# Block attention with decay and a Gelu MLP on one core: a hand-ordered two-stream pipeline, with q, k, v loaded as float32 through SyncE's queue

## The chip, the core and the metric

The kernel runs on one core of a Trainium2 chip. A core has a matrix engine (TensorE: PE for matmuls, PEld for weight loads), three engines for elementwise work (VectorE or DVE, ScalarE or ACT, GpSimd or POOL) and SyncE (SP), which here only issues DMAs. Each engine works through its own instructions in order and waits on semaphores for the others. Matmul results land in PSUM, eight banks of 2 KB per partition; all other tiles lie in SBUF. DMAs are issued from a queue of SP or of POOL, and the loads from POOL may change the type on the way (float32 in memory, bf16 in SBUF).

The metric is the device time of one execution in microseconds, the median of several runs. A profile of one execution gives the spans and waits.

## What is computed

```python
def _attn_ref(q, k, v, lam):                 # q, k, v: (4, 8, 768, 64) float32
    ...
    for b in range(nb):
        sl = slice(b * block, (b + 1) * block)
        qb, kb, vb = (q[:, :, sl], k[:, :, sl], v[:, :, sl])
        intra = np.einsum('bhic,bhjc->bhij', qb, kb) * Dmask[None]
        intra = np.einsum('bhij,bhjd->bhid', intra, vb)
        inter = np.einsum('bhid,bhde->bhie', qb * lam_pow[None], kv_state)
        out[:, :, sl] = intra + inter
        rev_pow = lam[:, None, None] ** (block - 1 - pos[None, :, None])
        kb_dec = kb * rev_pow[None]
        kv_state = lam_block[None, :, None, None] * kv_state + np.einsum('bhsd,bhse->bhde', kb_dec, vb)

def _moe_ref(x, w_in, w_out):                # x: (3072, 512), w_in: (512, 2048), w_out: (2048, 512)
    h = x @ w_in
    g = 0.5 * h * (1.0 + erf(h * inv_sqrt2))
    return g @ w_out
```

Four batches of eight heads run causal attention with a decay `lam` per head, carried from block to block in a state of 64 by 64 per head. The heads' outputs, side by side, are the 512 features of 3,072 tokens, which pass a two-layer MLP with an exact Gelu.

## The kernel before

The kernel cuts a batch of 768 tokens into six chunks of 128. For a chunk, `attn_batch` multiplies q by `lam**pos` (`q_hat`, line 104) and k by `lam**-pos` (`k_hat`, line 105) on POOL, which makes the decay between two tokens a plain product. PE transposes both for pairs of heads (lines 112 and 113), DVE copies the two results out of PSUM (116, 117), PE forms the scores of eight heads (124), and DVE applies the causal mask while copying (`sc_m`, 130). Then PE makes the output, transposed, from the masked scores and v (135) and from q and the state of the earlier chunks (136), and ACT copies it into `xT_sb` (138), which holds the MLP's input for all tokens. The chunk's addition to the state is eight small matmuls (143), two DVE adds on the diagonal blocks (151, 152) and one DVE multiply by `lam**128` (153); two POOL memsets (149, 150) clear the blocks off the diagonal in the new state tile. The chain from `sc_m` to the output and the state to the next chunk is serial.

`moe_chunk` takes 256 tokens. For each of 16 blocks of 128 hidden features it runs four matmuls of 256 columns into `h_ps` (162; two buffers), a Gelu on ACT into `gT` (165), and two matmuls of 512 columns that add this block's share to two output banks (167). At the end ACT copies both banks (171) and SP stores them (172).

The program is traced batch by batch: attention of a batch, then its three MLP chunks. The Tile framework's scheduler orders the instructions of each engine by its own priorities and dependences, so attention of the next batch is moved among the matmuls of the MLP before. q, k and v of a batch come as three DMAs on POOL's queue (94 to 96), which turn float32 into bf16 and land in one tile per tensor; the tiles have two buffers. The weights are two more such DMAs, traced after batch 0 (180, 181). POOL therefore does the multiplies and issues all loads in one order, and SP only stores.

Of the kernel before, what the change touches and what calls it, by code (L numbers as in the profile page):

```python
# [8 lines left out]
F32 = mybir.dt.float32  # L10
BF16 = mybir.dt.bfloat16
I32 = mybir.dt.int32
ALU = mybir.AluOpType
# [4 lines left out]
def kernel(  # L18
# [10 lines left out]
    nc = tc.nc  # L29
# [3 lines left out]
    n_tokens = B * S  # L33
    C = 128
    NB = S // C
    assert d_model == H * D

    TOK = 256
    NK1 = d_model // 128
    NK2 = d_ff // 128  # L40
    NO = TOK // 128

    xT_pool = ctx.enter_context(tc.tile_pool(name="xTp", bufs=1))
    xT_sb = xT_pool.tile([128, d_model // 128, n_tokens], BF16)

    consts = ctx.enter_context(tc.tile_pool(name="consts", bufs=1))

    lam_b = consts.tile([128, H], F32)
    nc.sync.dma_start(lam_b, lam[None, :].to_broadcast((128, H)))
    ln_lam = consts.tile([128, H], F32)  # L50
    nc.scalar.activation(ln_lam, lam_b, ACT.Ln)
# [4 lines left out]

    lam_pos = consts.tile([128, H], F32)
    nc.vector.tensor_scalar(lam_pos, ln_lam, scalar1=pos, scalar2=None, op0=ALU.mult)
    nc.scalar.activation(lam_pos, lam_pos, ACT.Exp)

    lam_neg = consts.tile([128, H], F32)
    nc.vector.tensor_scalar(lam_neg, ln_lam, scalar1=pos, scalar2=-1.0, op0=ALU.mult, op1=ALU.mult)
    nc.scalar.activation(lam_neg, lam_neg, ACT.Exp)

    lam_blk = consts.tile([128, H, D], F32)
    nc.scalar.activation(lam_blk[:, :, :], ln_lam[:, :, None].to_broadcast((128, H, D)), ACT.Exp, scale=float(C))

# [3 lines left out]
    ident = consts.tile([128, 128], BF16)  # L71
    make_identity(nc, ident)
# [4 lines left out]
    lam_blk_hd = lam_blk.rearrange("p h d -> p (h d)")  # L77

    w_pool = ctx.enter_context(tc.tile_pool(name="w", bufs=1))
    w_in_t = w_pool.tile([128, d_model // 128, d_ff], BF16)  # L80
    w_out_t = w_pool.tile([128, d_ff // 128, d_model], BF16)

    qkv_pool = ctx.enter_context(tc.tile_pool(name="qkv", bufs=2))
    hat_pool = ctx.enter_context(tc.tile_pool(name="hat", bufs=2))
    work_pool = ctx.enter_context(tc.tile_pool(name="work", bufs=2))
    kv_pool = ctx.enter_context(tc.tile_pool(name="kv", bufs=2))
    g_pool = ctx.enter_context(tc.tile_pool(name="g", bufs=3))
    out_pool = ctx.enter_context(tc.tile_pool(name="outp", bufs=3))

    def attn_batch(b, psum):  # L90
        q_t = qkv_pool.tile([128, H, NB, D], BF16, tag="q")
        k_t = qkv_pool.tile([128, H, NB, D], BF16, tag="k")
        v_t = qkv_pool.tile([128, H, NB, D], BF16, tag="v")
        nc.gpsimd.dma_start(q_t, q[b].rearrange("h (so si) d -> si h so d", si=128))
        nc.gpsimd.dma_start(k_t, k[b].rearrange("h (so si) d -> si h so d", si=128))
        nc.gpsimd.dma_start(v_t, v[b].rearrange("h (so si) d -> si h so d", si=128))  # L96

        kv_state = kv_pool.tile([128, H * D], BF16)
        nc.vector.memset(kv_state, 0.0)

        for sb in range(NB):
            q_hat = hat_pool.tile([128, H, D], BF16, tag="qh")
            k_hat = hat_pool.tile([128, H, D], BF16, tag="kh")
            nc.gpsimd.tensor_mul(q_hat, q_t[:, :, sb, :], lam_pos_b)  # L104
            nc.gpsimd.tensor_mul(k_hat, k_t[:, :, sb, :], lam_neg_b)  # L105
            vb = v_t[:, :, sb, :]

            HP = H // 2
            qT_ps = psum.tile([128, HP * C], BF16, tag="qT")
            kT_ps = psum.tile([128, HP * C], BF16, tag="kT")  # L110
            for hp in range(HP):
# [102 lines left out]
```

## Time and profile before

| | |
|---|---|
| median of three runs | 297.76 us (297.51 to 354.67) |
| span of the profiled execution | 296.9 us |
| first matmul of the MLP (line 162) | starts at 37.1 us |
| last Gelu (line 165) | starts at 291.4 us |
| HBM read, written | 27.27 MB, 6.29 MB |
| DMA packets on POOL's queue | 76,512 (13.63 MB as landed) |
| mean granted TensorE clock | 0.960 |

The page of the profile covers one execution and has a span from the first to the last instruction; the time of a run is taken around the whole program, and the profiled execution's own time outside its span is not shown. In what follows, "idle before" is the time in which an engine had nothing running before an instruction, with the engine or DMA whose end released it. A matmul's duration includes its way through the array, so matmuls that start every 0.1 us each last longer than that; the distance between starts tells what PE can do. "L162" is line 162 of the kernel.

### The profile page before, as it was taken

The page shows a single profiled execution, that of the slowest core. Times are in us where ns is not written, and L with a number is a line of the kernel's source. Part 1 is how long each engine was busy: PE and PEld are TensorE (multiplying, and loading weights), DVE is VectorE, ACT ScalarE, POOL GpSimd, SP SyncE. Part 2 cuts the span into 40 slices and gives each one's busy share as a digit, 9 for nine tenths or more (in the row PEclk, how much of TensorE's full clock was granted, in tenths as well). Part 3 has the DMA queues.
Part 4 walks back from the last instruction along what each step waited for, and adds up shares of the span by engine and source line. Part 5 has one row for each costly group of instructions (what it writes and reads, how often), then busy time and mean ns, then how long its engine had stood idle before and what let it go on. Part 6 is the DMA issues. An engine that isn't in the chain of part 4 may idle for free.

```text
span 296.9 us, 5123 instructions
## 1 busy us (share of the span) xinstructions
PE 238.1 (80%) x2081; PEld 145.1 (49%) x2112; DVE 85.6 (29%) x150; ACT 103.8 (35%) x247; POOL 94.7 (32%) x119
## 2 busy tenths in 40 slices
PE   0037295999999789999999799999998789999893
PEld 0025162555555456655554555555555556555451
DVE  1037544400000679500000768300003778100000
ACT  4001221343344323353534223453533133453532
POOL 7474625847200778610000645300003531000000
PEclk9999997999999969999999879999999689999999
DMA  6996999999990194990010100010101000010101
GB/s 44 157 118 116 187 192 126 123 146 137 154 174 0 71 80 30 106 152 27 6 68 0 73 0 2 2 71 0 73 1 56 17 2 1 2 71 2 71 1 71
DMA packets 80135, 20.25 MB, mean 68 GB/s; under 512 B 74480, under 2 KB 76528, under 8 KB 80112
## 3 DMA queue, kind: packets, MB, share of 16 engines
q0 software_dynamic: 76512, 13.63, 67.0%
q1 hardware_dynamic: 3600, 6.30, 5.6%
q8 instruction: 16, 0.26, 0.4%
q14 instruction: 7, 0.06, 0.1%
HBM read 27.27 MB, written 6.29 MB: 113 GB/s over the span
## 4 chain that ended last, share of the span: by engine, by line
PE 60%; ACT 12%; DMA 9%; issue 7%; DVE 6%; POOL 4%; ACTq 1%; POOLq 0%
PE omps L167 32%; PE h_ps L162 16%; ACT gT L165 11%; DMA w_out_t<-in_moe_w_out_dram 5%; DMA k_t<-in_k_dram 4%; PE sc_ps L124 3%; PE out_ps L135 3%; DVE sc_m L130 3%; PE out_ps L136 2%; PE kT_ps L113 2%; POOL q_hat L104 1%; DVE kv_state_new L153 1%; PE qT_ps L112 1%; POOL k_hat L105 1%; PE kv_ps L143 1%
## 5 line engine op out<-in xcount | busy, mean ns | idle before, releaser
L162 PE MATMUL h_ps<-xT_sb,w_in_t 128*128 128x256 bf16 x768 | 116.4, 279 | 4.0 <-DMA w_in_t<-in_moe_w_in_dram 4.0
L167 PE MATMUL omps<-w_out_t,gT 128*128 128x512 bf16 x353 | 105.3, 386 | 15.8 <-ACT gT L165 4.4
L165 ACT ACTIVATE gT<-h_ps 128x256 bf16<-128x256 f32 x192 | 73.1, 384 | 127.2 <-PE h_ps L162 117.2
L162 PEld LDWEIGHTS <-w_in_t 128*128 128x128 bf16 x768 | 76.0, 100 | 42.1 <-DMA w_in_t<-in_moe_w_in_dram 4.3
L167 PEld LDWEIGHTS <-gT 128*128 128x128 bf16 x384 | 29.6, 98 | 50.6 <-ACT gT L165 35.9
L104 POOL TENSOR_TENSOR q_hat<-q_t,lam_pos 128x512 bf16<-128x512 bf16 x24 | 25.1, 1052 | 78.3 <-PE qT_ps L112 57.7
L116 DVE COPY qT<-qT_ps 128x512 bf16<-128x512 bf16 x24 | 10.1, 421 | 122.5 <-PE qT_ps L112 119.8
L130 DVE TENSOR_TENSOR sc_m<-sc_ps,cmask 128x1024 bf16<-128x1024 f32 x24 | 29.4, 1224 | 28.8 <-PE sc_ps L124 28.7
L105 POOL TENSOR_TENSOR k_hat<-k_t,lam_neg 128x512 bf16<-128x512 bf16 x24 | 25.7, 1071 | 34.5 <-PE kv_ps L143 26.9
L138 ACT CAST xT_sb<-out_ps 128x512 bf16<-128x512 f32 x24 | 14.0, 585 | 55.4 <-PE out_ps L136 55.4
L112 PE MATMUL qT_ps<-ident,q_hat 128*128 128x128 bf16 x96 | 12.3, 251 | 17.2 <-POOL q_hat L104 17.1
L135 PE MATMUL out_ps<-sc_m,v_t 128*64 128x128 bf16 x192 | 16.5, 248 | 7.2 <-DVE sc_m L130 6.0
L153 DVE TENSOR_TENSOR kv_state_new<-kv_state_new,lam_blk 128x512 bf16<-128x512 bf16 x24 | 18.0, 749 | 1.8
L112 PEld LDWEIGHTS <-q_hat 128*128 128x128 bf16 x96 | 7.9, 111 | 19.8 <-POOL q_hat L104 17.6
L124 PE MATMUL sc_ps<-qT,kT 64*128 64x128 bf16 x192 | 11.4, 247 | 5.7 <-DVE kT L117 5.4
L149 POOL MEMSET kv_state_new<- 64x256 bf16 x24 | 7.3, 306 | 27.0 <-PE out_ps L136 26.3
L135 PEld LDWEIGHTS <-v_t 128*64 128x64 bf16 x192 | 12.9, 125 | 5.7 <-issue 5.3
L113 PE MATMUL kT_ps<-ident,k_hat 128*128 128x128 bf16 x96 | 11.8, 245 | 3.6 <-POOL k_hat L105 2.5
L171 ACT COPY out_sb<-omps 128x512 f32<-128x512 f32 x24 | 12.9, 589 | 4.8 <-PE omps L167 4.6
L136 PE MATMUL out_ps<-qT,kv_state_new 128*64 128x128 bf16 x160 | 13.6, 245 | 0.0
L117 DVE COPY kT<-kT_ps 128x512 bf16<-128x512 bf16 x24 | 10.1, 420 | 11.0 <-PE kT_ps L113 10.6
L96 POOL DMA_DIRECT2D v_t<-in_v_dram x4 | 8.9, 2225 | 12.8 <-DMA q_t<-in_q_dram 6.0
(35 smaller groups left out, 100.1 us busy)
## 6 DMA issues: line engine op xcount, KB each, us to landing
out_dram<-out_sb SPq DMA_DIRECT2D x24, 256.0 KB, 2.2
q_t<-in_q_dram POOLq DMA_DIRECT2D x4, 768.0 KB, 9.5
k_t<-in_k_dram POOLq DMA_DIRECT2D x4, 768.0 KB, 11.6
v_t<-in_v_dram POOLq DMA_DIRECT2D x4, 768.0 KB, 10.8
w_in_t<-in_moe_w_in_dram POOLq DMA_DIRECT2D x1, 2048.0 KB, 13.5
w_out_t<-in_moe_w_out_dram POOLq DMA_DIRECT2D x1, 2048.0 KB, 15.1
lam_b<-in_lam_dram SPq DMA_DIRECT2D x1, 4.0 KB, 2.5
```

Of the source, the lines that this page charges most:

```text
L104: nc.gpsimd.tensor_mul(q_hat, q_t[:, :, sb, :], lam_pos_b)
L105: nc.gpsimd.tensor_mul(k_hat, k_t[:, :, sb, :], lam_neg_b)
L112: nc.tensor.transpose(qT_ps[:, hp * C:(hp + 1) * C], q_hat[:, 2 * hp:2 * hp + 2, :], ident)
L113: nc.tensor.transpose(kT_ps[:, hp * C:(hp + 1) * C], k_hat[:, 2 * hp:2 * hp + 2, :], ident)
L124: nc.tensor.matmul(sc_ps[:, (hi * HP + hp) * C:(hi * HP + hp + 1) * C], kT[hi * D:(hi + 1) * D, hp * C:(hp + 1) * C], qT[hi * D:(hi + 1) * ...
L130: nc.vector.tensor_mul(sc_m, sc_ps.rearrange("p (h c) -> p h c", h=H), cmask_b)
L135: nc.tensor.matmul(osl, vb[:, h, :], sc_m[:, hi * HP + hp, :], start=True, stop=False)
L136: nc.tensor.matmul(osl, kv_state[:, h * D:(h + 1) * D], qT[:, hp * C:(hp + 1) * C], start=False, stop=True)
L153: nc.vector.tensor_mul(kv_state_new, kv_state_new, lam_blk_hd)
L162: nc.tensor.matmul(h_ps, w_in_t[:, ki, kf * 128:(kf + 1) * 128], x_t[:, ki, :], start=(ki == 0), stop=(ki == NK1 - 1))
L165: nc.scalar.activation(gT, h_ps, ACT.Gelu)
L167: nc.tensor.matmul(om[io], gT[:, io * 128:(io + 1) * 128], w_out_t[:, kf, :], start=(kf == 0), stop=(kf == NK2 - 1))
```

## The change

The scheduler is switched off (`manual_schedule`), and the order of every engine is written out. Attention chunks are numbered 0 to 23, and the MLP is cut into groups of 6, 2, 4, 4, 4 and 4 chunks, 768 to 256 tokens. Chunks 0 to 5 run first. Then, while the MLP of a group runs, the attention of the next group's chunks is placed between its matmul blocks, in four steps (`hats`, `transposes`, `scores`, `outputs`) at fixed shares of the group's PE work.

- **Loads.** q, k and v go through SP's queue as float32 without a change of type, in pieces of one chunk and one tensor: 128 tokens by 8 heads by 64, 1,024 rows of 256 bytes. Batches 0 and 1 are issued at the start, batches 2 and 3 when the chunk that opens the batch before is prepared. The weights stay on POOL's queue, in eight slices, after chunk 1.
- **Rounding.** `q_hat` is rounded by its multiply as before. k is not scaled any more but rounded by a DVE copy (`k_bf`); instead v is scaled by `lam**-pos` on POOL (`v_hat`), which serves both the output and the state.
- **State.** Two fixed tiles, cleared once, take turns; the memsets per chunk are gone. Both heads of a pair share one output matmul against the state, so four instead of eight. The multiply by `lam**128` moves from DVE to POOL in two halves. The state's addition is left out for a batch's last chunk, and the state's term for its first.
- **Copies.** q and k transposed leave PSUM in one copy of 1,024 elements instead of two of 512. The output's copy moves from ACT to DVE (`x_t`).
- **MLP.** All first-layer blocks of a group come first, with 384, 256 or 512 columns, and the Gelu results stay in SBUF (`g_t`); then each 128 tokens gets its 16 second-layer matmuls in a row.

```diff
+    groups = [6, 2, 4, 4, 4, 4]
...
+    ctx.enter_context(tc.manual_schedule())
...
+    def load_piece(b, name, lo, hi):
+        src = dict(q=q, k=k, v=v)[name]
+        for so in range(lo, hi):
+            nc.sync.dma_start(
+                qkv[b, name][:, so, :, :],
+                src[b, :, so * C:(so + 1) * C, :].rearrange("h si d -> si h d"))
...
+    def load_weights():
+        for s in range(NS):
+            f = d_ff // NS
+            nc.gpsimd.dma_start(w_in_t[:, :, s * f:(s + 1) * f], w_in_r[:, :, s * f:(s + 1) * f])
...
+    def hats(n):
...
+        nc.vector.tensor_copy(c.k, qkv[c.b, "k"][:, c.sb, :, :])
...
+        nc.gpsimd.tensor_mul(c.q_hat, qkv[c.b, "q"][:, c.sb, :, :], lam_pos_b)
+        nc.gpsimd.tensor_mul(c.v_hat, qkv[c.b, "v"][:, c.sb, :, :], lam_neg_b)
...
+    def transposes(c):
+        t_ps = ps.tile([128, 2, HP * C], BF16, tag="t", name="t_ps")
...
+        nc.vector.tensor_copy(c.qkT, t_ps)
...
+    def scores(c):
+        sc_ps = ps.tile([128, H, C], F32, tag="sc", name="sc_ps")
+        kv_ps = ps.tile([128, HP, D], F32, tag="t", name="kv_ps")
...
+        nc.vector.tensor_mul(c.sc_m, sc_ps, cmask_b)
...
+                    nc.vector.tensor_add(new[p, :, p], c.state[p, :, p], kv_ps[p, :, :])
...
+                    nc.gpsimd.tensor_mul(new[p, :, p], new[p, :, p], lam_blk_r[p, :, hi, :])
...
+    def outputs(c, x_t, off):
+        o_ps = ps.tile([128, HP, C], F32, tag="o", name="o_ps")
...
+        nc.vector.tensor_copy(x_t[:, :, off * C:(off + 1) * C], o_ps)
...
+                h_ps = ps.tile([128, N], F32, tag="mh", name="h_ps", bufs=2)
...
+        blocks = [(mm1(kf, sub), 4 * N) for kf in range(NK2) for sub in range(nsub)]
+        blocks += [(mm2(io, part), 4 * 512) for io in range(m) for part in range(NK2 // 4)]
...
+    for n in range(groups[0]):
+        transposes(live[n])
+        if n + 1 < groups[0]:
+            live[n + 1] = hats(n + 1)
+        scores(live[n])
+        outputs(live[n], xT[0], n)
+        if n == 1:
+            load_weights()
+    load_batch(1)
...
+            first = 0.45 if g == 0 else 0.0
...
+                todo += [(at(-0.3), 0, step), (at(0.05), 1, step), (at(0.4), 2, step), (at(0.75), 3, step)]
```

POOL's order at the start. Before, the three loads of batch 0 stand ahead of the first multiplies, and the weights come later one by one:

```order
L94 DMA q_t<-in_q_dram 128x48x64
L95 DMA k_t<-in_k_dram 128x48x64
L96 DMA v_t<-in_v_dram 128x48x64
L104 TENSOR_TENSOR q_hat<-q_t,lam_pos 128x512
L105 TENSOR_TENSOR k_hat<-k_t,lam_neg 128x512
```

After, from the hats of chunk 2 on:

```order
L143 TENSOR_TENSOR q_hat<-q_t,lam_pos 128x512
L144 TENSOR_TENSOR v_hat<-v_t,lam_neg 128x512
L184 TENSOR_TENSOR state_117<-state_117,lam_blk 64x4x64 x2
L125 DMA w_in_t<-in_moe_w_in_dram 128x4x512 x4
L128 DMA w_out_t<-in_moe_w_out_dram 128x4x512 x4
L143 TENSOR_TENSOR q_hat<-q_t,lam_pos 128x512
L144 TENSOR_TENSOR v_hat<-v_t,lam_neg 128x512
```

The loads of q, k and v have left POOL, and the eight weight DMAs now stand together between the state multiplies of chunk 1 and the hats of chunk 3.

DVE's order for one chunk of the first batch. Before, from the mask of the second chunk (the second instruction of a pair follows where the add has two halves):

```order
L130 TENSOR_TENSOR sc_m<-sc_ps,cmask 128x1024
L151 TENSOR_TENSOR kv_state_new<-kv_state_new,kv_ps 64x4x64
L152 TENSOR_TENSOR kv_state_new<-kv_state_new,kv_ps 64x4x64
L116 COPY qT<-qT_ps 128x512
L153 TENSOR_TENSOR kv_state_new<-kv_state_new,lam_blk 128x512
L117 COPY kT<-kT_ps 128x512
```

After, the same chunk:

```order
L154 COPY qkT<-t_ps 128x1024
L140 CAST k_bf<-k_t 128x512
L171 TENSOR_TENSOR sc_m<-sc_ps,cmask 128x1024
L180 TENSOR_TENSOR state_117<-state_119,kv_ps 64x4x64 x2
L196 CAST x_t<-o_ps 128x4x128
```

The multiply of the state is gone from DVE, the output's copy has come, and the rounding of the next chunk's k, which waits for its piece, stands ahead of this chunk's mask.

PE's order in the MLP, with buffer numbers. Before, in a stretch without attention:

```order
L162 MATMUL h_ps_2425<-xT_sb_58,w_in_t_89 128x256
L167 LDWEIGHTS gT_2421
L167 MATMUL omps0_2324<-w_out_t_90,gT_2421 128x512
L167 LDWEIGHTS gT_2421
L167 MATMUL omps1_2325<-w_out_t_90,gT_2421 128x512
L162 LDWEIGHTS w_in_t_89
L162 MATMUL h_ps_2434<-xT_sb_58,w_in_t_89 128x256
L167 LDWEIGHTS gT_2430
L167 MATMUL omps0_2324<-w_out_t_90,gT_2430 128x512
```

After, where the last group passes from the first layer to the second:

```order
L211 MATMUL h_ps_2532<-x_t_2056,w_in_t_133 128x512
L211 LDWEIGHTS w_in_t_133
L211 MATMUL h_ps_2532<-x_t_2056,w_in_t_133 128x512
L223 LDWEIGHTS g_t_2441
L223 MATMUL o2_ps_2538<-w_out_t_134,g_t_2441 128x512
```

Before, the second-layer matmuls of a block follow its Gelu within a few matmuls; after, all 64 first-layer matmuls of the group stand ahead of its first second-layer matmul, which reads the Gelu of the group's first block.

275 lines of the change are left out of this document (164 added, 111 removed).

## The prediction

> **What bounds the kernel now.** I read the page's busy line first, then the busy time by batch, then the waits, then two stretches of the timeline. The busy line and four windows (one per batch of 768 tokens, cut where its MLP begins) come first; the columns of a window are its length, then busy time and count of PE, PEld, DVE, ACT, POOL, then the granted clock, the DMA share and GB/s.
>
> ```profile
> span 296.9 us, 5123 instructions
> PE 238.1 (80%) x2081; PEld 145.1 (49%) x2112; DVE 85.6 (29%) x150; ACT 103.8 (35%) x247; POOL 94.7 (32%) x119
> ...
> 37.00:98.70 61.70, 54.22 (x417) 32.29 (x425) 10.35 (x18) 22.63 (x57) 23.05 (x23) 0.97 1.64 127
> 98.70:163.50 64.80, 58.20 (x521) 35.61 (x528) 21.80 (x38) 24.36 (x61) 23.63 (x28) 0.95 0.64 62
> 163.50:227.80 64.30, 58.37 (x520) 35.89 (x528) 20.34 (x35) 25.08 (x61) 15.37 (x24) 0.95 0.07 26
> 227.80:292.40 64.60, 57.62 (x512) 34.87 (x519) 20.39 (x35) 24.73 (x61) 10.43 (x16) 0.95 0.07 26
> ```
>
> TensorE is the engine in use, and every batch costs about 64.5 us whether DMA is busy or not. So loads bound only the first 37 us. Inside a batch PE is shown busy, but a shown matmul includes its latency, so I looked at starts.
>
> ```profile
> 200.12 0.60 PE L167 MATMUL omps<-w_out_t,gT 128*128 128x512 bf16 x2
> ...
> 201.11 0.93 PE L162 MATMUL h_ps<-xT_sb,w_in_t 128*128 128x256 bf16 x7
> 201.69 0.82 ACT L165 ACTIVATE gT<-h_ps 128x256 bf16<-128x256 f32 x2 [1.19 <-PE h_ps L162]
> 202.13 0.11 PEld L167 LDWEIGHTS <-gT 128*128 128x128 bf16 x2 [0.38 <-ACT gT L165]
> ...
> L165 ACT ACTIVATE gT<-h_ps 128x256 bf16<-128x256 f32 x192 | 73.1, 384 | 127.2 <-PE h_ps L162 117.2
> L171 ACT COPY out_sb<-omps 128x512 f32<-128x512 f32 x24 | 12.9, 589 | 4.8 <-PE omps L167 4.6
> PEld L167 <- ACT gT L165: 35.9, 97, 0.8
> ```
>
> In pure MLP the pattern repeats from 200.12 to 202.13: 2.01 us for two blocks of d_ff. Seven first-layer matmuls in 0.93 us, one of them lasting about 0.27, start every (0.93-0.27)/6 = 0.11 us for 256 columns. Two blocks stream 4,096 columns, so 1.76 us. The other 0.25 us is the wait for a Gelu that the next matmuls need at once. One chunk of 256 tokens takes 16.1 us instead of 14.1, and three per batch take 48.3; the remaining 16 us of a batch go to six attention chunks, 2.7 us each, on PE.
>
> **The MLP stream.** The change puts all first-layer matmuls of a group ahead of all second-layer ones. Columns are unchanged: 1,536 pieces of 256 columns at 0.11 us = 169.0 us. What remains of the Gelu wait is the two h_ps buffers: block k+2 waits for the Gelu of block k. From the start of a block's last matmul to the first of block k+2 pass the matmul (0.38 us at 512 columns, row below), about 0.09 to ACT, a Gelu of 512 (estimated 0.59, as the 512-wide copy's 589 ns) and 0.06 back: 1.12 us, plus three pitches of 0.22, 1.78 us for two blocks against 1.76 of streaming. At 384 columns the same sum is 1.46 against 1.32, at 256 it is 1.13 against 0.88. Over 64, 32 and 16 blocks: 0.6 + 2.2 + 2.0 us, a part of the last covered by attention steps: 4 us. The ends are 0 and 5.
>
> ```profile
> L167 PE MATMUL omps<-w_out_t,gT x353: 376/379/631, 48.5 to 292.0; 128*128 128x512 bf16 x177
> ...
> 242.39 0.40 PE L124 MATMUL sc_ps<-qT,kT 64*128 64x128 bf16 x8
> 242.72 0.32 PE L143 MATMUL kv_ps<-v_t,k_hat 128*64 128x64 bf16 x8
> 242.96 0.40 PE L112 MATMUL qT_ps<-ident,q_hat 128*128 128x128 bf16 x4
> 243.20 0.82 PE L162 MATMUL h_ps<-xT_sb,w_in_t 128*128 128x256 bf16 x6
> 244.43 0.25 PE L135 MATMUL out_ps<-sc_m,v_t 128*64 128x128 bf16 x2 [0.42 <-ACT gT L165]
> ...
> 244.85 0.23 PE L136 MATMUL out_ps<-qT,kv_state_new 128*64 128x128 bf16 x2
> ```
>
> **Attention inside the stream.** Start to start, eight score matmuls take 0.33 us, eight state matmuls 0.24, four transposes 0.24. The sixteen half-width output matmuls start about 0.028 us apart; the change keeps eight (0.23) and makes the other eight into four of full width (4 x 0.055 = 0.22). A chunk is then 0.48 + 0.33 + 0.24 + 0.45 = 1.50 us of PE, and 18 chunks lie in the stream: 27 us. Their other work is hidden as long as each PE step comes later than its inputs: in groups of 512 tokens steps stand 0.35 x 7 = 2.4 us or more apart, and the longest link is the 1.22 us mask below. DVE per chunk is about 3.8 us and POOL 3.2 (two 1.05 us multiplies, two state multiplies of half size), against 8 us of PE. Group 1 squeezes four chunks into one 256-token MLP; steps are 1.2 us apart there while scores to outputs needs 1.7, about 0.5 us four times and a little at the transposes: 3 us.
>
> **The start.** Six chunks now run before any MLP, each PE step waiting for DVE.
>
> ```profile
> 14.08 1.05 POOL L104 TENSOR_TENSOR q_hat<-q_t,lam_pos 128x512 bf16<-128x512 bf16 x1
> 19.92 0.61 PE L112 MATMUL qT_ps<-ident,q_hat 128*128 128x128 bf16 x4 [1.01 <-POOL q_hat L104]
> 20.46 0.61 PE L124 MATMUL sc_ps<-qT,kT 64*128 64x128 bf16 x8
> 27.04 1.23 DVE L130 TENSOR_TENSOR sc_m<-sc_ps,cmask 128x1024 bf16<-128x1024 f32 x1 [0.44 <-PE sc_ps L124]
> 28.18 0.40 DVE L151 TENSOR_TENSOR kv_state_new<-kv_state_new,kv_ps 64x256 bf16<-64x256 bf16 x1
> ...
> 31.61 1.23 DVE L130 TENSOR_TENSOR sc_m<-sc_ps,cmask 128x1024 bf16<-128x1024 f32 x1 [0.71 <-PE sc_ps L124]
> 37.12 1.89 PE L162 MATMUL h_ps<-xT_sb,w_in_t 128*128 128x256 bf16 x8 [3.99 <-DMA w_in_t<-in_moe_w_in_dram]
> 5.35 0.19 ACT L59 ACTIVATE lam_pos<-lam_pos 128x8 f32<-128x8 f32 x1
> L116 DVE COPY qT<-qT_ps 128x512 bf16<-128x512 bf16 x24 | 10.1, 421 | 122.5 <-PE qT_ps L112 119.8
> L180 POOL DMA_DIRECT2D w_in_t<-in_moe_w_in_dram x1: 815/815/815, 23.5 to 23.5; - x1
> ```
>
> Before, the first multiply waited for q to 14.08; now the first pieces are small and lam_pos (done at 5.54 there, about 5.1 with its turn moved up) is last. Then: q_hat to 6.2, eight transposes at the slow pitch of 0.10 us to 7.2, one copy of both (0.42 doubled less its fixed part, about 0.7) to 8.0, scores to 8.7, mask to 10.0. A chunk's period alone: mask 1.22, two state adds 0.82 (they free the bank that the next transposes need), transposes 1.05, copy 0.7, scores 0.62, and four hand-overs: 4.75 us, against 4.57 us between the masks at 27.04 and 31.61. Six chunks end their masks at 10.0 + 5 x 4.75 = 33.8. The eight weight DMAs stand on POOL behind the second state multiplies (about 16.7 us) and ahead of the hats of chunk 3; at 0.8 us of issue each they hold POOL to 23.2, q_hat is done at 24.3 instead of before 20.4, and the chain slips 3.9 us. With outputs and the copy to x_t the MLP starts at 33.8 + 3.9 + 1.5 = 39.2 us. That is no earlier than now: the change buys the stream, not the start.
>
> **What loading costs.**
>
> ```profile
> 6.00:8.00 2.00, 0.00 (x0) 0.00 (x0) 0.00 (x0) 0.00 (x0) 0.43 (x1) 1.00 2.43 155
> 10.00:12.00 2.00, 0.00 (x0) 0.00 (x0) 0.00 (x0) 0.00 (x0) 0.15 (x1) 1.00 2.45 157
> q_t<-in_q_dram POOLq DMA_DIRECT2D x4, 768.0 KB, 9.5
> w_in_t<-in_moe_w_in_dram POOLq DMA_DIRECT2D x1, 2048.0 KB, 13.5
> L172 SPq DMA_DIRECT2D out_dram<-out_sb x24: 332/332/1218, 66.7 to 293.3; - x24
> DMA to landing us min/median/max: 2.0/2.2/6.1
> 48.50:52.50 4.00, 3.73 (x27) 1.79 (x28) 0.32 (x2) 1.17 (x3) 0.30 (x1) 0.60 1.90 121
> ```
>
> A piece is 1,024 rows of 256 bytes; 18 pieces per batch, 72 in all, on SP, with landing waits eight pieces back. No row shows that form on SP. From below: at 155 GB/s of bf16 written, the same 1,024 rows (128 KB) pass in 0.85 us. From above: SP issues 128 rows in 0.33 us, and if issue grew with rows, 2.66 us. The chunk chain needs three pieces per 4.75 us, so any price under about 1.5 us is hidden. The POOL queue's issue grows far less than its rows, and bytes must pass anyway, so I take 1.0 us; batch 0 has then landed near 21 us, and nothing is paid. The weights (13.5 us for the first on an idle queue) land during the start and the first layer. Rounding of k on DVE (about 0.42 us) hides behind the scores, but stands ahead of the mask: k of the next chunk late means this chunk late. The two 64-partition memsets per chunk disappear from POOL, which was no bound. One warm-up remains: around 48.5 us the clock was 0.60 for 4 us, 2 us lost; PE works in fits at the start here too, so I keep 2.
>
> **Sum.** 39.2 (start) + 169.0 (MLP columns) + 27 (18 chunks) + 4 (Gelu) + 3 (group 1) + 2 (clock) + 4.5 (last matmul at 292.4 to the end at 296.9, unchanged) = 248.7 us of span. The profiled span is 296.9 and the median of the runs 297.76, 0.9 us more; with it 249.6 us.
>
> **Rivals.** One: loads pace the start. At 2.65 us a piece the k of chunk 5 lands near 48 us, its mask ends near 55, the MLP starts at 56 and the kernel takes 267. Half of that comes from milder causes, such as weights sharing the DMA engines with late pieces after 17 us: 258. For it: no row of that form; against it: 155 GB/s with 256-byte reads.
>
> By the Trainium skill, page "DMA: Bandwidth & Descriptors", section "Anatomy of one DMA", one DMA takes about 2.0 us plus its bytes over 436 GB/s, and the rules there ask for 1 MiB or more per DMA, which speaks against pieces: an estimated 2.6 us for one of 256 KB, and about the 267 us above if pieces went one behind the other. The trace of before speaks against such a gap: the flow is 155 GB/s at 6 us, in q, and 157 at 10 us, in k.
>
> Two: attention still costs PE 2.7 us a chunk inside the stream, because in-order waits or the dipping clock (0.95 in those windows) come back: 18 x 1.2 = 22 us more, 271; half of it 260. Against it: the steps are spaced over other matmuls.
>
> Three, slower: SP's queue limits the whole kernel. All batches pass it in order, and after the last piece some 42 us remain (a chunk, the last group's 28 us, the end). 72 pieces + 45 us reach 297 at 3.5 us a piece, a third above my upper bound. At 4 us: 333.
>
> Four, better: no POOL slip, no Gelu wait, a warm clock: 240.
>
> **Chances.** Forecast (244 to 255) 0.50; rival one 0.21; two 0.16; three 0.05; four 0.08. The range runs from four's 240 to near the full price of one, 267; it leaves out three and the tail of two. A change under 2% of 297.8 (6 us) is about what this measurement cannot tell from none: only a mix of one and two, or three near its threshold, ends there, 0.03. Faster 0.92, slower 0.05.
>
> **What would show it.** First L211 matmul near 39 us; SP issues of about 1 us or less, all of batch 0 landed before 22 us; a gap on POOL-fed transposes at chunk 3; in the last group a second-layer pitch of 0.22 us without waits; no more than 0.1 us of PE wait per block on Gelu; granted clock above 0.97. If the first L211 starts past 45 us, the load price was wrong; if the stretch from it to the last matmul exceeds 215 us, the stream was.

## The result, and the profile after

The changed kernel takes 261.1 us (median of 4 runs, 259.27 to 262.23) against 298.26 us for the kernel before on the same chip: a ratio of 0.876, 95% interval 0.871 to 0.881. One of the four runs of the kernel before took 354.67 us, far off its others, and is left out of the ratio. The 261.1 lies in the range given (240 to 267) and 11.5 us above the forecast of 249.6. The profiled execution took 260.31 us with a span of 258.5, so 1.8 us lie outside the span, where the forecast had 0.9. (The kernel before has the same 1.8 us: a run of 298.29 has a span of 296.5. The 0.9 came of setting the span of one run against the median of several.)

From the page of the changed kernel: the span, the busy line, and the chain that ended last, by engine.

```profile
span 258.5 us, 3976 instructions
PE 219.9 (85%) x1648; PEld 116.1 (45%) x1648; DVE 91.7 (35%) x140; ACT 78.9 (31%) x143; POOL 78.3 (30%) x97
...
PE 57%; SPq 32%; POOL 3%; issue 2%; DMA 2%; DVE 1%; ACT 0%; ACTq 0%; POOLq 0%
```

The busy line looks like a kernel bound by TensorE throughout. The chain says otherwise: 32% of the span, some 83 us, hang on SP's queue. Two places in the timeline show how. The first is the start. These are rows of SP, DVE, POOL and PE between 17 and 47 us (start, duration, engine, instruction; in brackets the idle time before it and what ended it).

```profile
18.83 1.32 SPq L66 DMA_DIRECT2D k_t<-in_k_dram  x1
20.19 5.53 SPq L66 DMA_DIRECT2D v_t<-in_v_dram  x1
25.76 6.60 SPq L66 DMA_DIRECT2D q_t<-in_q_dram  x1
32.41 6.46 SPq L66 DMA_DIRECT2D k_t<-in_k_dram  x1
...
17.59 3.16 POOL L125 DMA_DIRECT2D w_in_t<-in_moe_w_in_dram  x4
...
24.88 0.61 PE L150 MATMUL t_ps<-ident,q_hat 128*128 128x128 bf16 x4 [3.81 <-POOL q_hat L143]
...
36.15 0.43 DVE L140 CAST k_bf<-k_t 128x512 bf16<-128x512 f32 x1 [4.88 <-DMA k_t<-in_k_dram]
...
42.86 1.04 POOL L144 TENSOR_TENSOR v_hat<-v_t,lam_neg 128x512 bf16<-128x512 f32 x1 [11.00 <-DMA v_t<-in_v_dram]
...
45.33 0.61 PE L190 MATMUL o_ps<-qkT,state 128*128 128x128 bf16 x4 [4.29 <-POOL state L184]
...
46.44 5.79 PE L211 MATMUL h_ps<-x_t,w_in_t 128*128 128x384 bf16 x19
```

SP issues pieces at about 1.15 us until the weights, issued on POOL from 17.59, are in flight; then one piece takes 5.5 to 6.6 us. Several pieces are on their way at a time, so a piece lands well after it is issued: the k_t and v_t of chunk 5 are the ones issued at 18.83 and 20.19, and what waits for them starts at 36.15 and 42.86. The slip at chunk 3 is there as worked out (3.81 us). But the late pieces hold up chunk 5: its v_t delays `v_hat` of chunk 5, and with it the state multiply behind `v_hat` on POOL, for which PE waits 4.29 us; the MLP starts at 46.44 instead of 39.2.

The second place is the end of group 0, at 80 to 98 us: SP's queue, ACT's copies out of PSUM, and PE.

```profile
85.89 1.12 SPq L66 DMA_DIRECT2D v_t<-in_v_dram  x1
87.11 11.62 SPq L229 DMA_DIRECT2D out_dram<-o_sb  x6
...
83.51 0.58 ACT L227 COPY o_sb<-o_ps 128x512 f32<-128x512 f32 x1 [3.31 <-PE o_ps L223]
93.46 1.20 ACT L227 COPY o_sb<-o_ps 128x512 f32<-128x512 f32 x2 [9.37 <-DMA out_dram<-o_sb]
...
94.10 3.61 PE L223 MATMUL o_ps<-w_out_t,g_t 128*128 128x512 bf16 x16 [2.47 <-ACT o_sb L227]
```

The first store of group 0 stands on SP behind all 18 pieces of batch 2, so behind 54 pieces in all, and is issued at 87.11. There are three o_sb buffers; the fourth copy waits 9.37 us for the first store, and PE 2.47 us for the copy. It looks small. The experiments show that it decides what an earlier start is worth.

Behind that, TensorE runs as forecast. The last group:

```profile
226.67 13.98 PE L211 MATMUL h_ps<-x_t,w_in_t 128*128 128x512 bf16 x64
240.48 13.98 PE L223 MATMUL o_ps<-w_out_t,g_t 128*128 128x512 bf16 x64
```

64 matmuls of 512 columns start in 240.48 - 226.67 = 13.81 us, a pitch of 0.216 us without any wait, and the last one ends at 240.48 + 13.98 = 254.46.

| term of the sum | forecast, us | measured, us |
|---|---|---|
| start to the first L211 | 39.2 | 46.4 |
| MLP columns (768 of 512 columns at 0.216) | 169.0 | 165.7 |
| 18 chunks of attention on PE | 27 (1.50 each) | 30.2 (1.68 each) |
| Gelu waits, group 1, cold clock | 4 + 3 + 2 | 9.6 |
| PE waits for the copy of group 0 | 0 | 2.5 |
| last matmul to the end of the span | 4.5 | 4.0 |
| outside the span | 0.9 | 1.8 |

The 9.6 is what remains of the 208.0 us from 46.44 to 254.46. Of it 3.4 are three waits for q_hat in the stretch of group 1, and 2.3 the first four blocks of the MLP, whose Gelus start 1.28 us apart instead of 0.70. The other 3.9 stand against the 4 us forecast for Gelus, but only some 1.5 can be seen as such: in group 0 the Gelus start 0.70 us apart on average where four matmuls of 384 columns need 0.65. The rest was not traced.

### The profile page after: what moved, and what is told of

Read it like the earlier page. It is cut to its first block, busy times and chain, and to the rows that moved or that the text cites. A ratio compares the mean times of both kernels' runs of the same rounds, so it can differ in the third digit from the quotient of the medians.

```text
span 258.5 us, 3976 instructions
## 1 busy us (share of the span) xinstructions
PE 219.9 (85%) x1648; PEld 116.1 (45%) x1648; DVE 91.7 (35%) x140; ACT 78.9 (31%) x143; POOL 78.3 (30%) x97
## 4 chain that ended last, share of the span: by engine, by line
PE 57%; SPq 32%; POOL 3%; issue 2%; DMA 2%; DVE 1%; ACT 0%; ACTq 0%; POOLq 0%
SPq L66 32%; PE o_ps L223 25%; PE h_ps L211 23%; DMA out_dram<-o_sb 2%; PE sc_ps L161 2%; PE o_ps L194 2%; POOL state L184 2%; PE t_ps L150 2%; PE t_ps L152 1%; POOL q_hat L143 1%; PE kv_ps L168 1%; PE o_ps L190 1%; DVE sc_m L171 1%; DVE state L180 0%; ACT o_sb L227 0%
## 5 line engine op out<-in xcount | busy, mean ns | idle before, releaser
L211 PE MATMUL h_ps<-x_t,w_in_t 128*128 128x512 bf16 (+2 forms) x448 | 92.4, 356 | 0.1
L223 PE MATMUL o_ps<-w_out_t,g_t 128*128 128x512 bf16 x384 | 88.1, 379 | 2.5 <-ACT o_sb L227 2.5
L213 ACT ACTIVATE g_t<-h_ps 128x512 bf16<-128x512 f32 (+2 forms) x112 | 60.0, 536 | 82.4 <-PE h_ps L211 82.0
L211 PEld LDWEIGHTS <-w_in_t 128*128 128x128 bf16 x448 | 42.7, 99 | 39.7 <-issue 5.5
L184 POOL TENSOR_TENSOR state<-state,lam_blk 64x256 bf16<-64x256 bf16 x32 | 22.0, 687 | 113.1 <-DVE state L180 111.8
L223 PEld LDWEIGHTS <-g_t 128*128 128x128 bf16 x384 | 35.6, 98 | 42.3 <-issue 2.4
L154 DVE COPY qkT<-t_ps 128x1024 bf16<-128x1024 bf16 x24 | 16.6, 692 | 61.3 <-PE t_ps L152 61.3
L144 POOL TENSOR_TENSOR v_hat<-v_t,lam_neg 128x512 bf16<-128x512 f32 x24 | 25.0, 1042 | 17.7 <-DMA v_t<-in_v_dram 17.7
L143 POOL TENSOR_TENSOR q_hat<-q_t,lam_pos 128x512 bf16<-128x512 f32 x24 | 25.1, 1044 | 8.4 <-DMA q_t<-in_q_dram 3.6
L196 DVE CAST x_t<-o_ps 128x512 bf16<-128x512 f32 x24 | 16.6, 692 | 20.4 <-PE o_ps L194 20.0
L194 PE MATMUL o_ps<-sc_m,v_hat 128*64 128x128 bf16 x192 | 11.3, 246 | 8.3 <-DVE sc_m L171 8.2
## 6 DMA issues: line engine op xcount, KB each, us to landing
q_t<-in_q_dram SPq DMA_DIRECT2D x24, 256.0 KB, 5.1
k_t<-in_k_dram SPq DMA_DIRECT2D x24, 256.0 KB, 5.1
v_t<-in_v_dram SPq DMA_DIRECT2D x24, 256.0 KB, 5.1
out_dram<-o_sb SPq DMA_DIRECT2D x24, 256.0 KB, 2.0
```

The lines of the kernel that those rows point to most:

```text
L143: nc.gpsimd.tensor_mul(c.q_hat, qkv[c.b, "q"][:, c.sb, :, :], lam_pos_b)
L144: nc.gpsimd.tensor_mul(c.v_hat, qkv[c.b, "v"][:, c.sb, :, :], lam_neg_b)
L154: nc.vector.tensor_copy(c.qkT, t_ps)
L184: nc.gpsimd.tensor_mul(new[p, :, p], new[p, :, p], lam_blk_r[p, :, hi, :])
L194: nc.tensor.matmul(o_ps[hi * D:(hi + 1) * D, hp, :], c.v_hat[:, h, :], c.sc_m[:, hi * HP + hp, :], start=(c.sb == 0 and hp == 0), stop=Tru ...
L211: nc.tensor.matmul(h_ps, w_in_t[:, ki, kf * 128:(kf + 1) * 128], x_t[:, ki, sub * N:(sub + 1) * N], start=(ki == 0), stop=(ki == NK1 - 1))
```

## The experiments

Each set of runs was made on one chip with its own runs of the kernel before; the ratio in the table is against those. "MLP start" is the first matmul of L211 (or its line there), "copy wait" PE's longest wait for the copy out of PSUM, both from the profile. The span is that of the profiled run, the median that of all runs; the profiled run of e12 was its slowest, 241.73 us.

| run | MLP start | copy wait | span | median us | ratio to before (95%) |
|---|---|---|---|---|---|
| changed kernel | 46.44 | 2.47 | 258.5 | 261.1 | 0.876 (0.871 to 0.881) |
| e1, weights later | 39.62 | 8.68 | 259.3 | 261.98 | 0.878 (0.874 to 0.882) |
| e2, hats earlier | 40.91 | 7.13 | 259.3 | 260.72 | 0.873 (0.870 to 0.876) |
| e3, slip alone | 42.76 | 7.9 | 261.1 | 264.06 | 0.885 (0.881 to 0.889) |
| e4, short weight rows | 57.29 | 0 | 265.9 | 267.94 | 0.899 (0.895 to 0.902) |
| e5, stores on ACT | 46.89 | 0 | 256.0 | 257.68 | 0.864 (0.858 to 0.870) |
| e6, hats earlier and stores on ACT | 40.95 | 0 | 250.4 | 251.94 | 0.845 (0.841 to 0.850) |
| e7, casting loads | 59.14 | 0 | 284.0 | 285.51 | 0.955 (0.947 to 0.963) |
| e8, MLP interleaved | 46.63 | 0 | 261.3 | 262.44 | 0.881 (0.876 to 0.886) |
| e9, six groups of 512 | 29.55 | 0 | 239.4 | 241.54 | 0.809 (0.804 to 0.813) |
| e10, e6 and MLP interleaved | 40.86 | 0 | 276.6 | 278.61 | 0.932 (0.928 to 0.937) |
| e11, MLP in pairs | 46.37 | 0 | 272.6 | 274.44 | 0.921 (0.917 to 0.925) |
| e12, e9 with one slice earlier | 26.61 | 0 | 239.9 | 239.11 | 0.803 (0.799 to 0.807) |

### Do the weights slow the pieces, and does it matter? (e1 to e4)

**e1.** The weights move three chunks later:

```
-        if n == 1:
+        if n == 4:
             load_weights()
```

> The eight weight transfers move on POOL from behind chunk 1 to behind chunk 4, after the multiplies of chunk 5. Theory (weights share the DMA engines with the last pieces of batch 0 and slow them sixfold): all 18 pieces of batch 0 are issued at 1.4 us or less each and have landed by 26 us, the POOL slip of 3.8 us is gone too, the masks keep their 4.6 us period, and the MLP starts at about 36 us, held only by the first w_in slice (issued near 29.5, landing 6.7 later); time about 250 us. Rival (SP's queue itself becomes slow after some 18 pieces, weights or not): pieces issued after 20 us still take 5 us or more, MLP start 43 or later, 256 us or more.

The pieces did what the theory said. SP issues all pieces of batch 0 at 0.4 to 1.3 us each, and slows down only at 34.07 (but for one piece of 2.31), once the weights of this run are in flight. The MLP starts at 39.62, 6.8 us earlier than in the changed kernel though 3.6 later than expected; PE's last 4.74 us before it are a wait for the first w_in slice. Yet the time is the same. SP's queue, PE's timeline, and the window from 92 to 97 us of this run (its last three figures are granted clock, DMA share and GB/s):

```profile
32.91 1.11 SPq L66 DMA_DIRECT2D q_t<-in_q_dram  x1
34.07 6.30 SPq L66 DMA_DIRECT2D k_t<-in_k_dram  x1
40.41 6.74 SPq L66 DMA_DIRECT2D v_t<-in_v_dram  x1
...
88.67 10.88 SPq L229 DMA_DIRECT2D out_dram<-o_sb  x6
...
39.62 22.62 PE L211 MATMUL h_ps<-x_t,w_in_t 128*128 128x384 bf16 x115 [4.74 <-DMA w_in_t<-in_moe_w_in_dram]
...
93.57 4.96 PE L223 MATMUL o_ps<-w_out_t,g_t 128*128 128x512 bf16 x16 [8.68 <-ACT o_sb L227]
...
92.00:97.00 5.00, 3.43 (x10) 1.28 (x10) 0.00 (x0) 1.17 (x2) 0.00 (x0) 0.57 0.46 176
```

SP comes to the first store at 88.67, 1.6 us later than in the changed kernel, since the same 54 pieces and the same weights have to pass first in whatever order. What the start won is waited for at the copy: start -6.82, copy wait 8.68 - 2.47 = +6.21, and the sixteen matmuls behind the pause take 4.96 instead of 3.61 us, +1.35, at a granted clock of 0.57 in that window. Sum +0.7; the spans differ by +0.8. The theory was right about the pieces and wrong about the time.

That slow stretch agrees with the Trainium skill, page "TensorE: Matmul & The Clock Gate", section "Part 1: The HAM clock gate (the 'warmup' mystery)": an idle window of about 3.4 us puts the array to half rate. The pause of 8.68 us was followed by the lower clock, the one of 2.47 us in the changed kernel was not (1.00 from 93.9 to 97.5).

**e2.** The hats are issued two chunks ahead instead of one:

```
     live[0] = hats(0)
+    live[1] = hats(1)
...
-        if n + 1 < groups[0]:
-            live[n + 1] = hats(n + 1)
+        if n + 2 < groups[0]:
+            live[n + 2] = hats(n + 2)
```

> The weight transfers stay where they are, but the hats of each chunk are issued one chunk earlier, so that q_hat and v_hat of chunk 3 stand ahead of the weights on POOL. Theory (the slowed pieces set the start, not the slip): the slip at chunk 3 goes, but v_t of chunk 5 still lands near 43 us, the MLP starts at 44 to 46.5 us and the time is 259 to 261. Rival (the POOL slip is what cost): MLP start near 42.5, 257 us or less.

The MLP starts at 40.91 and the time is 260.72. The time lies in the forecast range by luck, since the start was missed: with two hats in front POOL reaches the weights only at 21.29 instead of 17.59, so more pieces pass before them. The run therefore does not separate the slip from the slowed pieces. But it is a second case of an early start (5.5 us) without a gain: PE waits 7.13 us for the copy.

```profile
93.01 5.49 PE L223 MATMUL o_ps<-w_out_t,g_t 128*128 128x512 bf16 x16 [7.13 <-ACT o_sb L227]
```

**e3.** POOL's issues without the weights' bytes (the small transfers fill a tile that nothing reads):

```
         if n == 1:
-            load_weights()
+            few = consts.tile([128, 2 * NS, NK1, 8], BF16)
+            for s in range(2 * NS):
+                nc.gpsimd.dma_start(few[:, s, :, :], w_in_r[:, :, s * 8:(s + 1) * 8])
+        if n == 4:
+            load_weights()
```

> Behind chunk 1 stand eight transfers of the same 512 rows, but of 32 bytes read per row, and the real weights go behind chunk 4. Theory: POOL's slip of about 3.8 us stays without the weights' bytes; pieces of batch 0 keep 1.4 us or less, chunk 3 to 5 run 3.8 us late but else at 4.6 us, the first w_in slice lands near 40 us and the MLP starts there; 253 to 254 us, some 4 us above the run with the weights only moved. Rival (contention is by rows or descriptors, not by bytes, or SP's queue is slow by itself): pieces issued during or after these transfers take 3 us or more, MLP start 43 or later, 257 us or more.

Pieces take 1.25 to 2.56 us while the small transfers pass, so 512 rows of 32 bytes disturb little. The MLP starts at 42.76, 3.1 us behind e1, which is the price of the slip (3 to 4 us expected). The forecast of 253 fails as in e1: PE waits 7.9 us for the copy, and the time is 264.06.

**e4.** As e2, with each weight transfer cut in two along its rows:

```
-        for s in range(NS):
-            f = d_ff // NS
+        for s in range(2 * NS):
+            f = d_ff // (2 * NS)
...
+            for e in range(2):
+                nc.gpsimd.dma_start(w_out_t[:, s * f:(s + 1) * f, e * 256:(e + 1) * 256],
+                                    w_out_r[:, s * f:(s + 1) * f, e * 256:(e + 1) * 256])
```

> As the run with earlier hats, but each weight transfer is cut in two along the row: 16 transfers of 512 rows of 1 KB. Theory (the engines take rows of the two queues in turn, so a piece's share grows as the other's rows shrink): a piece issued while weights are in flight takes 3 to 3.5 us instead of 6, all of batch 0 has landed by 34 us; POOL is held 12 us by the issues, which then is the limit for chunk 4, MLP start 40 to 42, 254 to 256 us. Rival (shares go by bytes or by queue): pieces still take about 6 us, and the time is 259 us or more.

SP's queue and POOL's, in the stretch with weights in flight:

```profile
42.28 4.13 SPq L66 DMA_DIRECT2D k_t<-in_k_dram  x1
46.45 4.13 SPq L66 DMA_DIRECT2D v_t<-in_v_dram  x1
...
32.33 0.74 POOL L129 DMA_DIRECT2D w_out_t<-in_moe_w_out_dram  x1 [1.46 <-DMA w_in_t<-in_moe_w_in_dram]
34.44 0.74 POOL L129 DMA_DIRECT2D w_out_t<-in_moe_w_out_dram  x1 [1.37 <-DMA w_in_t<-in_moe_w_in_dram]
36.63 0.74 POOL L129 DMA_DIRECT2D w_out_t<-in_moe_w_out_dram  x1 [1.45 <-DMA w_in_t<-in_moe_w_in_dram]
```

A piece now takes 4.13 us where it took 6.46 beside rows of 2 KB: the share follows the length of the other queue's rows. POOL's issues, each released by the landing of an earlier transfer of 512 rows, stand 2.11 and 2.19 us apart, so in 4.13 us some 980 weight rows pass beside the 1,024 rows of the piece: nearly row for row. The changed kernel gives the same estimate: from 25 to 45 us 195 to 197 GB/s land, of which a piece every 6.5 us makes 40; the other 155 are some 990 weight rows, each 1 KB as landed, per piece. The size was missed (3 to 3.5 us expected), and POOL's side wholly: from the ninth transfer on, POOL waits at each issue for an earlier one to land, so the hats of chunk 4 come at 43.86, the state multiply behind them makes PE wait 19.7 us, and the MLP starts at 57.29.

By the Trainium skill, page "DMA: Bandwidth & Descriptors", section "Queues, rings and completion order", a DMA engine goes round-robin between the queues that have work for it, a packet at a time. The counts above agree with equal turns; how many rows make a turn is not to be seen in these runs.

### Is it the stores? (e5, e6)

The edit of e5 alone; e6 has it and the edit of e2:

```
-                    nc.sync.dma_start(out[r:r + C, :], o_sb)
+                    nc.scalar.dma_start(out[r:r + C, :], o_sb)
```

> The changed kernel, with the 24 stores issued from ACT's queue instead of SP's. New theory after the first four runs: SP works without a pause until 87 to 90 us to pass three batches of q, k, v, the first store of group 0 stands behind them, and the fourth copy of group 0 waits for that store's buffer; so whatever the start gains is given back there. Here the MLP still starts at 46.4, only the 2.5 us wait for the copy goes: 257 to 259 us. Rival (the copy's wait is hidden, or stores from ACT hold the Gelus up): 260 us or more.

> Hats one chunk earlier and stores on ACT's queue together. New theory: the earlier MLP start (41.4 us, 5 us gained) is no longer given back, the 7.1 us wait for the copy is gone: 252.5 to 254.5 us. Rival (loads or the state chain limit group 0 and 1 anyway): 257 us or more, with a new wait on k_t, q_t or v_t in group 1.

Both came nearly as forecast: 257.68, and 251.94 where 252.5 to 254.5 was expected. PE's wait for the copy is gone in both. From the page of e6: the chain that ended last, and the row of the second-layer matmuls, whose last figure, PE's idle time before them, is 2.5 us in the changed kernel:

```profile
PE 78%; POOL 7%; DVE 4%; issue 3%; SPq 3%; DMA 2%; ACT 1%; ACTq 0%; POOLq 0%; DVEq 0%
...
L223 PE MATMUL o_ps<-w_out_t,g_t 128*128 128x512 bf16 x384 | 88.1, 380 | 0.0
```

SP's queue has 3% of the chain instead of 32%. From e5's span of 256.0 to e6's 250.4 are 5.6 us, the 5.9 by which the MLP starts earlier; on SP the same edit of the hats had given nothing (e2). So what held the time was the place of the stores: behind 54 loads on SP's queue an early start cannot count, with the stores elsewhere it counts in full. The wait is for one of three o_sb buffers; whether more buffers would do as well was not tried.

### What the loading path is worth (e7)

```
-            qkv[b, name] = qkv_pool.tile([128, NB, H, D], F32, tag=name, name=f"{name}_t")
+            qkv[b, name] = qkv_pool.tile([128, H, NB, D], BF16, tag=name, name=f"{name}_t")
...
-            nc.sync.dma_start(
-                qkv[b, name][:, so, :, :],
-                src[b, :, so * C:(so + 1) * C, :].rearrange("h si d -> si h d"))
+        nc.gpsimd.dma_start(
+            qkv[b, name][:, :, lo:hi, :],
+            src[b, :, lo * C:hi * C, :].rearrange("h (so si) d -> si h so d", si=C))
...
-        for so in range(NB):
-            for name in "qkv":
-                load_piece(b, name, so, so + 1)
+        for name in "qkv":
+            load_piece(b, name, 0, NB)
```

> The changed kernel with q, k, v loaded as bf16 by POOL's casting transfers: batch 0 in 18 pieces, two chunks ahead, the other batches by one transfer per tensor as in the kernel before. Stores stay on SP, which has nothing else to do. Theory: the f32 path through SP is worth something at the start alone, where POOL now issues 18 pieces of about 0.85 us beside hats and weights, some 6 us a chunk instead of 4.6: MLP start 47 to 51 us; the copy's 2.5 us wait goes; stream 205: 258 to 263 us, so the loading path by itself is worth within 3 us. Rival (loading as f32 through SP carries a large part of the gain): 268 us or more.

285.51 us: the theory fell, by 22 us beyond its upper end. POOL's queue of this run at 27 to 34 us, and PE where it waits later:

```profile
27.92 0.89 POOL L65 DMA_DIRECT2D q_t<-in_q_dram  x1 [1.05 <-DMA w_in_t<-in_moe_w_in_dram]
30.49 0.87 POOL L65 DMA_DIRECT2D k_t<-in_k_dram  x1 [1.68 <-DMA w_in_t<-in_moe_w_in_dram]
33.01 0.87 POOL L65 DMA_DIRECT2D v_t<-in_v_dram  x1 [1.65 <-DMA w_in_t<-in_moe_w_in_dram]
...
85.76 0.40 PE L146 MATMUL t_ps<-ident,q_hat 128*128 128x128 bf16 x4 [4.15 <-POOL q_hat L139]
...
147.71 0.61 PE L146 MATMUL t_ps<-ident,q_hat 128*128 128x128 bf16 x4 [8.47 <-POOL q_hat L139]
```

The issue of a piece was sized about right (0.87 to 0.94 us). What was left out is that POOL works in order: loads behind the weights wait for weights to land, and the multiplies of q_hat and v_hat stand behind the loads. The MLP starts 12.7 us later, and 4.15 and 8.47 us are lost where batches 2 and 3 are issued ahead of the hats, 25.3 us together. After each of these two pauses the granted clock is 0.60 and 0.59 for 4.3 us, an estimated 3.5 us more, and the copy wait of 2.5 us is saved: 26.3 against the 25.5 us between the spans. In this order of POOL's work the f32 path through SP is worth 24 us, because it takes the loads out of the way of POOL's multiplies. How much of it a better order on POOL would win back was not tried.

### What the order of the MLP is worth (e8, e10, e11)

**e8** keeps everything but the layers' order: 256 tokens at a time, the second layer one block behind.

```
+        for sub in range(T // N):
+            blocks.append((mm1(0, sub), 4 * N))
+            for kf in range(NK2):
+                if kf + 1 < NK2:
+                    blocks.append((mm1(kf + 1, sub), 4 * N))
+                for io in (2 * sub, 2 * sub + 1):
+                    blocks.append((mm2(io, kf), 512))
```

> The changed kernel with the MLP's order undone: 256 tokens at a time, second layer one d_ff block behind the first, as before. Theory: a Gelu of 256 columns and its two hand-overs take about 0.6 us against 0.44 us of first-layer matmuls beside it, so each of 192 blocks costs 1.0 to 1.08 us instead of 0.87: 25 to 40 us more, 280 to 300 us, the larger part of the change's gain. Rival (the new chunk pipeline carries the gain): 268 us or less.

262.44 us: again the theory fell. **e11** keeps e8, but has the second layers of two blocks one first-layer matmul apart and seven first-layer matmuls behind them, as the trace of before showed:

```
+            for kf in range(0, NK2, 2):
+                blocks += second(kf)
+                if kf + 2 < NK2:
+                    blocks.append((mm1(kf + 2, sub, 0, 1), N))
+                blocks += second(kf + 1)
+                if kf + 2 < NK2:
+                    blocks += [(mm1(kf + 2, sub, 1, NK1), 3 * N), (mm1(kf + 3, sub), 4 * N)]
```

> The run with the MLP's order undone (256 tokens at a time, stores on SP), but with the second layers of two d_ff blocks placed one first-layer matmul apart and seven first-layer matmuls behind them, as the trace of before shows them. Theory: this order, and not the missing split into layers, cost the 0.25 us per pair of blocks before; 96 pairs give back 24 to 26 us: 284 to 290 us against 262.4. Rival (the order is no cause; the clock or the scheduler's attention steps were): 270 us or less.

PE in pure MLP, first of e8, then of e11:

```profile
214.00 0.60 PE L210 MATMUL h_ps<-x_t,w_in_t 128*128 128x256 bf16 x4
214.43 0.59 PE L222 MATMUL o_ps<-w_out_t,g_t 128*128 128x512 bf16 x2
214.87 0.60 PE L210 MATMUL h_ps<-x_t,w_in_t 128*128 128x256 bf16 x4
```

```profile
245.25 0.61 PE L227 MATMUL o_ps<-w_out_t,g_t 128*128 128x512 bf16 x2
245.69 0.27 PE L214 MATMUL h_ps<-x_t,w_in_t 128*128 128x256 bf16 x1
245.80 0.59 PE L227 MATMUL o_ps<-w_out_t,g_t 128*128 128x512 bf16 x2
246.23 0.93 PE L214 MATMUL h_ps<-x_t,w_in_t 128*128 128x256 bf16 x7
247.19 0.61 PE L227 MATMUL o_ps<-w_out_t,g_t 128*128 128x512 bf16 x2
```

In e8 a block takes 0.87 us, what its columns need, and PE waits 1.8 us for Gelus in the whole run: four first-layer matmuls and the second layer of the block before do cover a Gelu. In e11 a pair takes 1.94 us (245.25 to 247.19) against 1.74, near the 2.01 of the kernel before, and the span grows by 11.3 us, the time by 12.0, outside both theories. So the order is a cause, but not of the whole: 96 pairs at 0.20 us would be 19, and 24 to 26 were forecast. Where an attention step stands between the blocks it covers the Gelu; that part was not counted out. The split into layers over a whole group, with its wider blocks, is worth 5.3 us beyond e8 (its span against e5's, both without a wait for the copy; 4.8 by the medians).

**e10** was to isolate that split on top of e6, with the edits of e8 and e6 together.

> The run with earlier hats and stores on ACT, with the MLP's order undone again (256 tokens at a time, second layer one block behind). Theory after the first such run: a hand-written lead of one block covers the Gelu, so splitting the layers over a whole group is worth nothing by itself: within 1.5 us of 251.9, 250.5 to 253.5 us. Rival (the split is worth some 4 us, which the first such run hid because its stores came early and met no wait): 255 to 258 us.

278.61 us, outside both theories. ACT's timeline of this run:

```profile
56.43 0.58 ACT L226 COPY o_sb<-o_ps 128x512 f32<-128x512 f32 x1 [0.48 <-PE o_ps L222]
65.55 0.38 ACTq L228 DMA_DIRECT2D out_dram<-o_sb  x1
65.96 0.58 ACT L226 COPY o_sb<-o_ps 128x512 f32<-128x512 f32 x1 [8.95 <-DMA v_t<-in_v_dram]
66.75 0.34 ACTq L228 DMA_DIRECT2D out_dram<-o_sb  x1
67.13 0.66 ACT L212 ACTIVATE g_t<-h_ps 128x256 bf16<-128x256 f32 x2 [0.58 <-DMA q_t<-in_q_dram]
```

The copy ends at 57.01, its store is issued at 65.55, and the trace puts the wait down to a piece of v_t: stores on ACT's queue, too, wait for load pieces. The Gelus stand behind the store, and PE waits 10.1 us for one. Ten more waits of 1.0 to 1.4 us come at later ends of 256 tokens, where two copies and two store issues stand ahead of the Gelus on ACT; over the run PE waits 22.6 us for Gelus, and the granted clock is 0.74 from 60 to 80 us, after the long wait. In e6 the same wait is there (a copy ends at 70.53, its store is issued at 74.18) and costs nothing, because the second-layer phase of a split group needs no new Gelu. So of these orders only the split hides the stores on ACT, and the run does not tell what the split is worth by itself.

### A kernel that beats both (e9, e12)

Stores on ACT, weights at n == 2, and:

```
-    groups = [6, 2, 4, 4, 4, 4]
+    groups = [4, 4, 4, 4, 4, 4]
```

> Six groups of 512 tokens instead of 768, 256 and four of 512; stores on ACT's queue; weights one chunk later on POOL (behind chunk 2, where the hats of the last chunk of the start are already issued). Theory: the MLP starts after four chunks, at 28 to 30 us, held by the chunk chain (25.7) or by the first w_in slice; the group of 256 tokens with its waits of 3.4 us is gone; 20 instead of 18 chunks lie in the stream at 1.7 us: 29 + 166 + 34 + 4 + 1.8 = 235, and up to 5 us more where chunks 6 and 7 wait for their pieces: 234 to 240 us. Rival (with less cover the loads of batch 1 limit group 1): waits of over 5 us on k_t, q_t or v_t in group 1 and 243 us or more.

241.54 us, 1.5 us above the range of the theory. The MLP starts at 29.55, after a wait of 3.82 us for the first w_in slice; the load waits of the rival did not come. The run changes three things at once, and their shares were not separated. e12 issues the first of the four w_in slices at n == 1 and the rest at n == 2:

```
-            load_weights()
+            load_weights(1, NS)
...
+        if n == 1:
+            load_weights(0, 1)
```

> As the run with six groups of 512, with the first of the four w_in slices issued one chunk earlier (behind chunk 1) than the rest. Theory: POOL slips by 0.8 us, the first slice lands by 25 us, the 3.8 us wait before the first L211 goes and the MLP starts at 26.5 to 27.5 us; the second slice, landing near 30, is needed then: 237.5 to 239.5 us against 241.5. Rival (the next slices now pace the first layer): the wait reappears at a later L211 and the time is 241 us or more.

239.11 us (238.23 to 241.73), a ratio of 0.803. The MLP starts at 26.61 as forecast, but in the profiled run PE waits 4.0 us for slices of w_out at 45 to 52 us, so the rival is right in part: the wait moves to a later slice, of w_out and not of w_in. The intervals of e9 and e12 overlap, on two chips; that e12 is the faster is not settled. Both are faster than the changed kernel by far more than that.

## Why the prediction was right in sign and 11.5 us too low

Of some 10.7 us by which the profiled run exceeds the forecast, 7.2 are the start, 3.0 the stream and 0.4 the end.

- **The start: 39.2 forecast, 46.4 measured.** The chain of six chunks was right to the slip: masks 4.6 us apart (4.75), POOL's slip 3.81 us (3.9). The step that failed is "batch 0 has then landed near 21 us, and nothing is paid". The free price of a piece was about right (1.0 taken, 1.15 measured), but beside the weights it is 6.5 us, far above the upper bound of 2.66, which was worked out for a queue alone. The estimated 2.6 us from a fixed part and the bytes was not the price either: the pieces flow at 1.15 us, several on their way at a time. This is the milder cause of rival one, put there at 258 us with a chance folded into 0.21.
- **What the prediction did not have at all** is the place of the stores. It asked of SP's queue only whether 72 pieces limit the end (rival three), not which instruction stands behind them earlier. e1 and e2 show what that meant: had the start come at 39.6 or 40.9, the time would still have been 261 to 262. So the forecast of 249.6 would have been missed with a perfect start too; e6, with the stores away from the loads and the MLP starting at 40.95, is 251.94.
- **The stream: 205 forecast, 208.0 measured.** The sum is right by luck, since its errors cancel. The columns were 3.3 us too dear (the 0.11 us pitch was read to two figures; it is 0.108), attention 3.2 us too cheap. Four full-width state matmuls take 0.32 us and not 0.22, and the eight half-width ones behind them 0.35 and not 0.23:

```profile
137.91 0.39 PE L190 MATMUL o_ps<-qkT,state 128*128 128x128 bf16 x4
138.23 0.41 PE L194 MATMUL o_ps<-sc_m,v_hat 128*64 128x128 bf16 x8
138.58 1.68 PE L211 MATMUL h_ps<-x_t,w_in_t 128*128 128x512 bf16 x7
```

- **Why the MLP gains.** The prediction gave about 20 us to putting all first-layer matmuls ahead (24 less the 4 left). The runs give 16.6: 11.3 for an order that leads by a whole block (e11 to e8) and 5.3 for the split over a group (e8 to e5). The gain is near in size; that the split was needed for all of it is not so. The rest of the stream's shortening, from 255.3 us before (37.12 to 292.4) to 222 in e11 (46.37 to 268), was not taken apart by a run. A part is no gain: before, only three of the 24 masks come ahead of 37.12, so its stream holds most of the work of 21 chunks, and now it holds 18, at the price of a later start. Two further changes are to be seen: 1.68 us of PE per chunk instead of the 2.7 that the prediction reckoned for the kernel before, and a granted clock of 1.00 instead of 0.95.
- **Group 1 and the clock.** 3 us of squeeze forecast, mostly four waits from scores to outputs; measured are 3.4 us, but in three waits for q_hat ahead of the transposes, behind two state multiplies of 0.69 us each on POOL, more than counted. The size is right, the place is not. 2 us for a warm-up, 2.3 measured at the first four blocks. The tail and the time outside the span are +0.4 together.
- **The signs named beforehand.** The first L211 past 45 us was to mean that the load price was wrong: it was, and SP's issues of about 1 us did not hold beside the weights. The others held: the gap at chunk 3, a second-layer pitch of 0.22 without waits, a clock above 0.97, a stream under 215 us.

## What to carry to other kernels

Before you credit an earlier start, follow every in-order queue to the first instruction that frees a buffer: a store that stands behind prefetches pins the time to when the prefetches have passed, however early its data are ready. The busy share of the bounding engine does not show this; the chain that ended last did, with a third of the span on the loading queue. And a price measured on a queue alone is not the price beside another queue: here the share went row for row, so pieces of short rows took 5.6 times as long beside long ones.

## What was not expected of the hardware

- Pieces of 1,024 rows of 256 bytes took 1.15 us alone, 6.46 beside rows of 2 KB and 4.13 beside rows of 1 KB on the other queue, while the total went down far less: 205 to 219 GB/s landed alone, 195 to 197 and 183 to 184 beside those rows.
- The first four MLP blocks start 1.28 us apart, against 0.70 later, though the profile shows a granted clock of 1.00 from 46.4 to 51.6 us; after the 8.68 us pause of e1 it shows 0.57. So the start of the kernel ran slow without the profile's clock saying so.
- With sixteen casting transfers on POOL, the ninth waited 0.29 us and those from the tenth on 1.4 to 1.7 us each for earlier ones to land (e4), and a store on ACT's queue waited 8.5 us with a load piece of SP's queue named as its releaser (e10).
